# Each 128-column product issued as two 64-column products in the two column halves of the matrix engine

## The chip, the cores and the metric

The kernel runs on one core of a Trainium2 chip. The metric is the device time of one execution in microseconds (us): the median of three runs. A core has a matrix engine (TensorE, PE in the profile), three engines for element-wise work (VectorE is DVE, ScalarE is ACT, GpSimd is POOL) and queues for transfers (DMA). The matrix engine holds a *stationary* operand, which a load (PEld) brings into its array, and streams a *moving* operand past it; the results go to PSUM.

## The reference

An attention block without softmax, then a mixture of four experts over its output. All is float32.

```python
# q, k, v: (8, 8, 576, 64); x: (4608, 512); w1: (4, 512, 1024); w2: (4, 1024, 512)
kv  = np.einsum('bhsd,bhse->bhde', k, v)
out = np.einsum('bhsd,bhde->bhse', q, kv)
rms = np.sqrt(np.mean(out * out, axis=-1, keepdims=True) + 1e-06)
attn = (out / rms * g_norm).astype(np.float32)
x = np.ascontiguousarray(attn.transpose(0, 2, 1, 3)).reshape(B * S, H * D)

p = domain_probs / (domain_probs.sum(-1, keepdims=True) + 1e-09)
out = np.zeros((N, D), dtype=np.float32)
for e in range(E):
    h = np.maximum(x @ w1[e], 0.0)
    out += p[:, e:e + 1] * (h @ w2[e])
```

Nearly all the arithmetic is in `x @ w1[e]` and `h @ w2[e]`.

## The kernel before

Python code first records all operations of the kernel (`plan.add`), each with an estimated cost for the engine it may run on, and a planner (`Plan.layout`) then lays them out: it fixes which engine does what, in which order, and in which buffer. The estimated costs steer only this order; they don't appear in the program. The work is cut into 36 steps, `s = e * 9 + c`: four experts `e` by nine chunks `c` of 512 rows. During the first nine steps (the first expert) the attention of the next batch runs between the products; the later 27 steps hold products alone.

Both large products are computed by a fast matrix multiplication (seven products in place of eight, in two levels for most steps), so the operands are sums and differences of blocks that the element-wise engines make ahead. A float32 product is issued by one call and shows as two records in the profile (two passes); a transpose shows as one.

The products that the change touches, with the shapes that matter (`P` is 128, `HN` 256, `NT` 512, `D` 64):

```python
def pe(products, columns, passes=2):                  # the planner's cost of products
    return {"PE": passes * products * (0.008 + 0.0008125 * columns) + 0.003}

# first product, two levels (steps 1 to 35), L962: 128 stationary, 128 moving columns
for i, m in enumerate(OUTER):                         # seven outer products
    for j, mm in enumerate(ORDER):                    # seven inner ones
        def product(eng, m=m, mm=mm, ps=ps):
            for u in range(2):
                nc.tensor.matmul(
                    ps.ap[:, u * P:(u + 1) * P],
                    lhsT=w1f[e][m][mm][1]()[:, u * P:(u + 1) * P], rhs=views[m][mm][1](),
                    start=(mm in (1, 5) and u == 0), stop=True, skip_group_check=True,
                )
        # ... ACT copies or DVE adds the bank's result into SBUF

# first product of step 0, plain, L1049: 512 moving columns
for kt in range(2):
    nc.tensor.matmul(
        bank.ap[:], lhsT=two(w.ap[:])[:, kt, ut * P:(ut + 1) * P],
        rhs=two(xh[dh].ap[:])[:, kt, :], ...)

# second product, one level (step 0, most of steps 1 to 7, step 35), L1179: 256 moving columns
for kt in range(4):
    nc.tensor.matmul(
        ps.ap[:, 0:HN], lhsT=four(h[m])[:, kt // 2, t, kt % 2, :],
        rhs=w2f[e][m].ap[:, kt * HN:(kt + 1) * HN], ...)

# second product, two levels (steps 8 to 34, a part of steps 1 to 7), L1262: 128 moving columns
for o, m in enumerate(group):
    b, at = forms[m][mm]
    for kt in range(2):
        col = at * HN + kt * P
        nc.tensor.matmul(
            ps.ap[:, o * P:(o + 1) * P], lhsT=b.ap[:, col:col + P],
            rhs=w2q[e][m][mm][1]()[:, kt, :], ...)
```

The attention, which the change leaves as it is, uses the array in parts already. Its products in the first nine steps (`...` marks cuts):

```python
# L683, batch 0 alone: q transposed by products of 64 stationary columns, in both column halves
for r in range(NR):
    for o in range(2):
        at = (o * NR + r) * D
        nc.tensor.matmul(
            bank.ap[o * D:(o + 1) * D, rs], lhsT=qt.ap[:, at:at + D], rhs=ident[:])
# L679, the other batches: full-array transposes of q
nc.tensor.transpose(bank.ap[:, rs], qt.ap[:, rs], ident[:])
# L702: k by v, 64 stationary and 64 moving columns, column half r
nc.tensor.matmul(
    bank.ap[r * D:(r + 1) * D, o * D:(o + 1) * D], lhsT=ks[r], rhs=vs[r], ...)
# L729 and L791: q by kv, in quarters of the array (64 rows, 64 columns)
nc.tensor.matmul(
    raw[r].ap[c * D:(c + 1) * D, ...], lhsT=qTs[hp].ap[half, at:at + D],
    rhs=kv.ap[half, o * D:(o + 1) * D])
# L747: full-array transposes of the attention's result; L773 and L807: transposes of 64 rows
# L1425: transposes of the identity, which keep PE at work while it would wait at the start
```

Of the kernel before, what the change touches and what calls it, by code (L numbers as in the profile page):

```python
# [234 lines left out]
def kernel(  # L235
# [36 lines left out]
    nc = tc.nc  # L272

    B, H, S, D = q.shape
    E, DM, F = moe_w1.shape
    P = nc.NUM_PARTITIONS
# [5 lines left out]
    HN = NT // 2  # L282
# [56 lines left out]
    plan = Plan()  # L339

    def pe(products, columns, passes=2):
        return {"PE": passes * products * (0.008 + 0.0008125 * columns) + 0.003}

    def dve(n):
        return {"DVE": 0.155 + 0.00104 * n}
# [65 lines left out]
    def two(ap):  # L411
        return ap.rearrange("p (k t) -> p k t", k=2)
# [519 lines left out]
    def up(s, e, views):  # L932
        made = {}
        h = {}

        def add(key, to, a, b, op=ALU.add, where=either):
            combine(
                key, where(2 * NT), lambda: to.ap[:], lambda: a.ap[:], lambda: b.ap[:], op,
                [a, b], [to],
            )  # L940

        def relu(key, b):
            plan.add(
                key, act(2 * NT),
                lambda eng: nc.scalar.activation(out=b.ap[:], in_=b.ap[:], func=ACT.Relu),  # L945
                reads=[b], writes=[b],
            )

        for i, m in enumerate(OUTER):
            n = f"{s}_{m}"  # L950
            whole = made[m] = Buf("big", f"m{n}")
            bank = {
                1: Buf("u1", f"u1_{n}"), 2: Buf("u2", f"u2_{n}"), 5: Buf("u2", f"u3_{n}"),
            }
            snap = {}
            for j, mm in enumerate(ORDER):
                key = s + (i + j / 7) / 7
                ps = bank[{2: 2, 5: 5, 3: 5}.get(mm, 1)]

                def product(eng, m=m, mm=mm, ps=ps):  # L960
                    for u in range(2):
                        nc.tensor.matmul(  # L962
                            ps.ap[:, u * P:(u + 1) * P],
                            lhsT=w1f[e][m][mm][1]()[:, u * P:(u + 1) * P], rhs=views[m][mm][1](),
                            start=(mm in (1, 5) and u == 0), stop=True, skip_group_check=True,
                        )

                op = plan.add(
                    key, pe(2, P), product,
                    reads=w1f[e][m][mm][0] + [views[m][mm][0]] + ([ps] if mm == 2 else []),  # L970
                    **{"parts" if mm == 2 else "writes": [ps]},
                    after=last[-2:-1] if mm == 1 else seeds if mm == 5 else (),
                )
                op.marks, op.seed = (ps, HN), mm == 2
                if mm == 3:
                    last.append(op)

                def copy(to, where, ps=ps, key=key):
                    return plan.add(
                        key - 0.4, act(HN),  # L980
                        lambda eng: nc.scalar.activation(  # L981
                            out=where(), in_=ps.ap[:, 0:HN], func=ACT.Copy),
                        reads=[ps], parts=[to],
                    )

                def total(a, t, src, add_, whole=whole, key=key):
                    plan.add(
                        key - 0.4, dve(HN),
                        lambda eng: nc.vector.tensor_tensor(  # L989
                            out=block(whole, a, t), in0=src.ap[:, 0:HN], in1=add_.ap[:], op=ALU.add),  # L990
                        reads=[src, add_], parts=[whole],
                    )

                if mm == 1:
                    seeds = [copy(bank[2], lambda b=bank[2]: b.ap[:, 0:HN])]
                elif mm in (6, 7):
                    snap[mm] = Buf("snap", f"s{mm}_{n}")
                    copy(snap[mm], lambda b=snap[mm]: b.ap[:])
                if mm == 2:
                    copy(whole, lambda whole=whole: block(whole, 0, 0))  # L1000
                elif mm == 7:
                    total(1, 1, bank[5], snap[7])
                elif mm == 4:
                    copy(whole, lambda whole=whole: block(whole, 1, 0))
                elif mm == 3:
                    total(0, 1, ps, snap[6])
            key = s + (i + 1) / 7

            def unit(f):
                h[f] = Buf("big", f"h{f}_{s}")  # L1010
                return h[f]

            if m == 2:
                add(key, unit(1), made[1], made[2])
                relu(key, h[1])
            elif m == 6:
                add(key, made[1], made[1], made[6])
            elif m == 5:
                add(key, made[6], made[1], made[5])
            elif m == 3:  # L1020
                add(key, unit(21), made[6], made[3])
                relu(key, h[21])
                add(key, unit(7), h[1], h[21], ALU.subtract)
            elif m == 7:
                add(key, made[1], made[1], made[7])
                add(key, unit(4), made[1], made[5], where=dve)
                relu(key, h[4])
                add(key, unit(5), h[21], h[4], where=dve)
                add(key, unit(6), h[5], h[1], ALU.subtract, dve)
            elif m == 4:  # L1030
                add(key, unit(2), made[1], made[4])
                relu(key, h[2])
                add(key, unit(3), h[2], h[6], ALU.subtract)
        hidden[s] = h

    def up_plain(s, e, c, key, span):
# [4 lines left out]
        for i in range(8):  # L1041
            uh, a, u = i // 4, i // 2 % 2, i % 2
            bank = Buf("u1" if a == 0 else "u2", f"up{s}_{i}")
            for dh in range(2):
                w, low = corners[uh, dh]

                def product(eng, w=w, bank=bank, dh=dh, ut=2 * a + u):
                    for kt in range(2):
                        nc.tensor.matmul(  # L1049
                            bank.ap[:], lhsT=two(w.ap[:])[:, kt, ut * P:(ut + 1) * P],  # L1050
                            rhs=two(xh[dh].ap[:])[:, kt, :], start=(dh == kt == 0),
                            stop=(dh == kt == 1), skip_group_check=True,
                        )

                op = plan.add(
                    key - 0.89 + 0.01 * (i ^ 2) if i < 4 and dh == 0 else key + span * i / 8,
                    pe(2, NT), product,
                    reads=[w, low, xh[dh]], **({"parts": [bank]} if dh else {"writes": [bank]}),
                )
                op.marks = bank, NT  # L1060
            for th, n in enumerate((1, 21) if uh == 0 else (2, 4)):
                plan.add(
                    key + span * i / 8, act(HN),
                    lambda eng, bank=bank, b=h[n], a=a, u=u, th=th: nc.scalar.activation(
                        out=four(b)[:, a, :, u, :], in_=two(bank.ap[:, th * HN:(th + 1) * HN]),
                        func=ACT.Relu,
                    ),
                    reads=[bank], parts=[h[n]],
                )
# [89 lines left out]
    def down(s, e, c, mixed=False):  # L1159
# [6 lines left out]
        for t in range(2):  # L1166
            banks = {}
            for j, m in enumerate(order):
# [7 lines left out]

                def product(eng, m=m, t=t, ps=ps):
                    for kt in range(4):
                        nc.tensor.matmul(  # L1179
                            ps.ap[:, 0:HN], lhsT=four(h[m])[:, kt // 2, t, kt % 2, :],  # L1180
                            rhs=w2f[e][m].ap[:, kt * HN:(kt + 1) * HN],
                            start=(m in (1, 2, 5) and kt == 0), stop=(kt == 3),
                            skip_group_check=True,
                        )
# [22 lines left out]
    def down_deep(s, e, c, groups=((1, 6), (7, 5), (4, 2), (3,)), base=None, h=None, merge=None, send=None):  # L1207
# [10 lines left out]
        for i, group in enumerate(groups):  # L1218
# [34 lines left out]
            for j, mm in enumerate(ORDER):  # L1253
# [3 lines left out]
                def product(eng, group=group, mm=mm, ps=ps, forms=forms):  # L1257
                    for o, m in enumerate(group):
                        b, at = forms[m][mm]
                        for kt in range(2):  # L1260
                            col = at * HN + kt * P
                            nc.tensor.matmul(  # L1262
                                ps.ap[:, o * P:(o + 1) * P], lhsT=b.ap[:, col:col + P],
                                rhs=w2q[e][m][mm][1]()[:, kt, :],
                                start=(mm in (1, 5) and o == 0 and kt == 0), stop=(kt == 1),
                                skip_group_check=True,
# [117 lines left out]
    for e in range(E):  # L1384
        for c in range(NCH):
# [19 lines left out]
            if s >= 1:  # L1405
                if not primed:
                    banks = [Buf("ab", f"prime{i}") for i in range(2)]

                    def prime(eng, banks=banks):
                        for b in banks:  # L1410
                            nc.tensor.matmul(b.ap[:, 0:P], lhsT=ident[:], rhs=ident[:], start=True,
                                             stop=False, skip_group_check=True)
                            nc.tensor.matmul(b.ap[:, P:HN], lhsT=ident[:], rhs=ident[:], start=False,
                                             stop=True, skip_group_check=True)

                    primed.append(plan.add(s + 1.1, pe(4, P), prime, writes=banks))
                    primed[0].marks = banks[0], HN
# [58 lines left out]
```

## Time and profile before

| | before |
|---|---|
| time, median of 3 runs | 1712.36 us (1711.51 to 1712.5) |
| span of the profiled execution | 1710.4 us |
| PE busy | 1700.4 us (99%) |
| DVE, ACT, POOL busy | 1276.0, 982.5, 715.0 us |
| PE records | 15630 products, 15630 loads |
| 128-column products: L962 | 6860 records in six groups |
| 128-column products: L1262 | 5684 records |

How to read it: the profile gives each engine's busy time and, for each group of instructions (line, engine, operation, output and inputs, shape), the count and the mean length. PE's records overlap: a product's record begins when it starts and ends when its result is through, while the next has long begun. So the length of a PE record is no cost; the distance from one start to the next is. The timeline shows groups in order of time with start, length from first start to last end, and count. "128*64" in a shape is rows by columns of the stationary operand, "128x128" behind it is the moving one.

### The profile page before, as it was taken

Reading aid. Unit: us, or ns where it says so; the run is one execution under the profiler, and the core shown is the slowest. Engines: PE = TensorE matmul, PEld = TensorE weight load, DVE = VectorE, ACT = ScalarE, POOL = GpSimd, SP = SyncE. Lnnn points to the kernel's source line nnn. Section 1 sums busy time; section 2 is a strip of 40 time slices with the busy share of each in tenths; the row PEclk is TensorE's granted clock in tenths of the full one; section 3 lists DMA queues with packets and bytes.
Section 4 is the critical chain, followed back from the end, with each engine's and each line's share of the span. In section 5 each row is a group of like instructions: output and inputs, shape, how many; then the busy total and the mean of one; then the engine's idle time right before and its main releaser. Section 6 shows DMA issues by size and latency. Waiting matters only on the chain.

```text
span 1710.4 us, 39615 instructions
## 1 busy us (share of the span) xinstructions
PE 1700.4 (99%) x15630; PEld 1647.5 (96%) x15630; DVE 1276.0 (75%) x2040; ACT 982.5 (57%) x2405; POOL 715.0 (42%) x677
## 2 busy tenths in 40 slices
PE   9999999999999999999999999999999999999998
PEld 6799999999999999999999999999999999999998
DVE  4855776677698787777788777777788887777774
ACT  3455555455456656665666666656566566656562
POOL 3634331323554543333355465333345544433331
PEclk9999999999999999999999999999999999999999
DMA  9964643544466344444577444444478444444442
GB/s 227 252 203 145 195 145 97 167 152 157 148 172 155 106 101 115 104 115 105 139 174 177 111 112 112 103 110 111 124 185 196 106 107 112 112 112 112 108 103 50
DMA packets 172225, 232.55 MB, mean 136 GB/s; under 512 B 61576, under 2 KB 112648, under 8 KB 172040
## 3 DMA queue, kind: packets, MB, share of 16 engines
q1 hardware_dynamic: 148968, 193.32, 37.3%
q0 software_dynamic: 23072, 36.71, 14.4%
q8 instruction: 123, 2.02, 0.5%
q14 instruction: 62, 0.51, 0.1%
HBM read 155.79 MB, written 74.19 MB: 134 GB/s over the span
## 4 chain that ended last, share of the span: by engine, by line
PE 97%; DVE 1%; DMA 1%; POOL 0%; issue 0%; SPq 0%; ACT 0%
PE u L962 45%; PE db L1262 23%; PE ab L1262 14%; PE db L1179 8%; PE u L1049 2%; PE ab L702 1%; DMA small<-in_q_dram 1%; PE ab L747 1%; PE ab L679 1%; DVE big L1131 1%; PE ab L729 1%; PE u L1179 1%; PE ab L1179 0%; PE ab L791 0%; POOL rt L587 0%
## 5 line engine op out<-in xcount | busy, mean ns | idle before, releaser
L365 DVE TENSOR_TENSOR big<-big,big 128x1024 f32<-128x1024 f32 (+1 forms) x537 | 506.5, 962 | 29.9 <-ACT big L945 15.2
L962 PE MATMUL u<-xf,big 128*128 128x128 f32 x3392 | 491.8, 275 | 0.0
L962 PEld LDWEIGHTS u<-xf,big 128*128 128x128 f32 x3392 | 435.9, 192 | 2.2
L962 PE MATMUL u<-xf,w1y 128*128 128x128 f32 x2652 | 391.5, 276 | 0.0
L989 DVE TENSOR_TENSOR big<-u,snap 128x256 f32<-128x256 f32 x462 | 194.3, 421 | 214.8 <-PE u L962 142.4
L962 PEld LDWEIGHTS u<-xf,w1y 128*128 128x128 f32 x2652 | 342.7, 192 | 1.9 <-DVE big L989 0.2
L981 ACT ACTIVATE snap<-u 128x256 f32<-128x256 f32 x490 | 187.5, 383 | 190.7 <-PE u L962 153.2
L365 POOL TENSOR_TENSOR big<-big,big 128x256 f32<-128x256 f32 (+1 forms) x168 | 215.9, 1299 | 168.2 <-DVE big L365 66.2
L981 ACT ACTIVATE big<-u 128x256 f32<-128x256 f32 x462 | 176.7, 383 | 103.3 <-PE u L962 72.9
L1262 PE MATMUL db<-big,big 128*128 128x128 f32 x1516 | 205.9, 275 | 0.0
L1262 PEld LDWEIGHTS db<-big,big 128*128 128x128 f32 x1516 | 187.3, 192 | 0.1
L365 POOL TENSOR_TENSOR big<-big 128x512 f32<-128x512 f32 (+1 forms) x87 | 105.5, 1215 | 142.2 <-DVE big L365 86.4
L1179 PE MATMUL db<-big,big 128*128 128x256 f32 x696 | 164.6, 380 | 0.0
L1290 ACT ACTIVATE snap<-db 128x256 f32<-128x256 f32 (+1 forms) x230 | 82.2, 357 | 116.8 <-PE db L1262 111.4
L945 ACT ACTIVATE big<-big 128x1024 f32<-128x1024 f32 x132 | 138.6, 1050 | 4.0 <-DVE big L365 3.3
L1179 PEld LDWEIGHTS db<-big,big 128*128 128x128 f32 x696 | 125.9, 191 | 13.9 <-DVE big L596 0.3
L1298 DVE TENSOR_TENSOR big<-ab,snap 128x256 f32<-128x256 f32 x164 | 69.1, 421 | 61.2 <-ACT snap L1290 29.9
L1328 POOL TENSOR_TENSOR big<-big 128x512 f32<-128x512 f32 x25 | 31.8, 1270 | 194.6 <-DVE big L365 174.9
L981 ACT ACTIVATE u<-u 128x256 f32<-128x256 f32 x245 | 90.9, 371 | 28.3 <-PE u L962 11.0
L1147 POOL DMA_DIRECT2D out_dram<-big x94 | 86.0, 1029 | 47.6 <-ACT big L1124 27.6
L365 DVE TENSOR_TENSOR big<-big 128x512 f32<-128x512 f32 (+1 forms) x120 | 105.4, 889 | 0.6 <-PE db L1179 0.6
L1262 PE MATMUL db<-kv,big 128*128 128x128 f32 x644 | 94.5, 275 | 0.0
(197 smaller groups left out, 2716.5 us busy)
## 6 DMA issues: line engine op xcount, KB each, us to landing
xf<-x SPq DMA_DIRECT2D x108, 512.0 KB, 3.7
out_dram<-big POOLq DMA_DIRECT2D x82, 256.0 KB, 5.8
xf<-x_h SPq DMA_DIRECT2D x81, 256.0 KB, 3.1
xf<-x SPq DMA_DIRECT2D x81, 256.0 KB, 3.5
x<-xf SPq DMA_DIRECT2D x36, 512.0 KB, 4.3
big<-in_moe_w_dram SPq DMA_DIRECT2D x31, 512.0 KB, 5.5
x_h<-big SPq DMA_DIRECT2D x18, 512.0 KB, 4.2
big<-in_moe_w_dram POOLq DMA_DIRECT2D x17, 512.0 KB, 6.1
```

Source lines behind the costliest of these rows:

```text
L365: lambda eng: adder(eng).tensor_tensor(out=out_(), in0=a(), in1=b(), op=op),
L945: lambda eng: nc.scalar.activation(out=b.ap[:], in_=b.ap[:], func=ACT.Relu),
L962: nc.tensor.matmul(ps.ap[:, u * P:(u + 1) * P], lhsT=w1f[e][m][mm][1]()[:, u * P:(u + 1) * P], rhs=views[m][mm][1](), start=(mm in (1, 5) ...
L981: lambda eng: nc.scalar.activation(out=where(), in_=ps.ap[:, 0:HN], func=ACT.Copy),
L989: lambda eng: nc.vector.tensor_tensor(out=block(whole, a, t), in0=src.ap[:, 0:HN], in1=add_.ap[:], op=ALU.add),
L1049: nc.tensor.matmul(bank.ap[:], lhsT=two(w.ap[:])[:, kt, ut * P:(ut + 1) * P], rhs=two(xh[dh].ap[:])[:, kt, :], start=(dh == kt == 0), stop ...
L1147: nc.gpsimd.dma_start(out=dst, in_=cell(i)[parts, :], accum_op=ALU.add)
L1179: nc.tensor.matmul(ps.ap[:, 0:HN], lhsT=four(h[m])[:, kt // 2, t, kt % 2, :], rhs=w2f[e][m].ap[:, kt * HN:(kt + 1) * HN], start=(m in (1, ...
L1262: nc.tensor.matmul(ps.ap[:, o * P:(o + 1) * P], lhsT=b.ap[:, col:col + P], rhs=w2q[e][m][mm][1]()[:, kt, :], start=(mm in (1, 5) and o == ...
L1290: lambda eng: nc.scalar.activation(out=where(), in_=group_of(ps.ap), func=ACT.Copy),
L1298: lambda eng: nc.vector.tensor_tensor(out=cell(tq, dq), in0=group_of(src.ap), in1=group_of(add_.ap), op=ALU.add,),
L1328: lambda eng: adder(eng).tensor_tensor(out=whole(to), in0=whole(a), in1=whole(b), op=ALU.add),
```

## The change

Every product with 128 stationary columns becomes two, each with 64 of these columns and with the output in the matching half of the PSUM partitions. The moving operand is the same for both. The aim is that each half of the array loads and streams on its own, so that one half's change of operand lies under the other's stream. The planner's cost of products is changed with it. Transposes and the attention's products stay as they were.

```diff
     def pe(products, columns, passes=2):
-        return {"PE": passes * products * (0.008 + 0.0008125 * columns) + 0.003}
+        return {"PE": passes * products * (0.0025 + columns / 1200.0) + 0.003}
+
+    def halves_of(out_, lhsT, rhs, **kw):
+
+        for half in range(2):
+            cols = slice(half * D, (half + 1) * D)
+            nc.tensor.matmul(out_[cols], lhsT=lhsT[:, cols], rhs=rhs, **kw)
@@ the first product, two levels
                     for u in range(2):
-                        nc.tensor.matmul(
+                        halves_of(
                             ps.ap[:, u * P:(u + 1) * P],
-                            lhsT=w1f[e][m][mm][1]()[:, u * P:(u + 1) * P], rhs=views[m][mm][1](),
+                            w1f[e][m][mm][1]()[:, u * P:(u + 1) * P], rhs=views[m][mm][1](),
                             start=(mm in (1, 5) and u == 0), stop=True, skip_group_check=True,
                         )
@@ the same edit in the plain first product (L1049), in both second products (L1179, L1262)
@@ and in the two pairs of priming products that clear two PSUM banks once
```

The planner's cost moves from 0.112 to 0.109 us for a pass of 128 columns and from 0.216 to 0.216 for 256, so the order it lays out changes in places as well.

More of the change, by code (lines that the diff above doesn't have):

```diff
@@ L1048, in product @@
                     for kt in range(2):
-                        nc.tensor.matmul(
-                            bank.ap[:], lhsT=two(w.ap[:])[:, kt, ut * P:(ut + 1) * P],
+                        halves_of(
+                            bank.ap[:], two(w.ap[:])[:, kt, ut * P:(ut + 1) * P],
                             rhs=two(xh[dh].ap[:])[:, kt, :], start=(dh == kt == 0),
@@ L1178, in product @@
                     for kt in range(4):
-                        nc.tensor.matmul(
-                            ps.ap[:, 0:HN], lhsT=four(h[m])[:, kt // 2, t, kt % 2, :],
+                        halves_of(
+                            ps.ap[:, 0:HN], four(h[m])[:, kt // 2, t, kt % 2, :],
                             rhs=w2f[e][m].ap[:, kt * HN:(kt + 1) * HN],
@@ L1261, in product @@
                             col = at * HN + kt * P
-                            nc.tensor.matmul(
-                                ps.ap[:, o * P:(o + 1) * P], lhsT=b.ap[:, col:col + P],
+                            halves_of(
+                                ps.ap[:, o * P:(o + 1) * P], b.ap[:, col:col + P],
                                 rhs=w2q[e][m][mm][1]()[:, kt, :],
@@ L1410, in prime @@
                         for b in banks:
[L1411 to L1414, printed above, removed]
+                            halves_of(b.ap[:, 0:P], ident[:], rhs=ident[:], start=True,
+                                      stop=False, skip_group_check=True)
+                            halves_of(b.ap[:, P:HN], ident[:], rhs=ident[:], start=False,
+                                      stop=True, skip_group_check=True)
                     primed.append(plan.add(s + 1.1, pe(4, P), prime, writes=banks))
```

## The prediction

> **What bounds the kernel now.** I read the page first: busy shares, slices, chain. TensorE (PE) is busy 99% of the span, its clock is granted in full throughout, and the chain that ended last is 97% PE, nearly all of it the three product lines L962, L1262 and L1179.
>
> ```profile
> PE 1700.4 (99%) x15630; PEld 1647.5 (96%) x15630; DVE 1276.0 (75%) x2040; ACT 982.5 (57%) x2405; POOL 715.0 (42%) x677
> PEclk9999999999999999999999999999999999999999
> PE 97%; DVE 1%; DMA 1%; POOL 0%; issue 0%; SPq 0%; ACT 0%
> ```
>
> There are 15630 PE records for 7994 products in the program: a float32 product is two records (two passes), a transpose one. So the time is the number of passes times the distance between two starts, and only that distance can move the end. A record's own length (275 ns) says nothing of it, since records overlap. I took the distance from the count of records in stretches that hold nothing but 128-column products (columns: stretch, then busy time and records of each engine, granted clock, DMA):
>
> ```profile
> 600.00:700.00 100.00, 100.00 (x898) 100.00 (x898) 76.38 (x118) 59.92 (x151) 37.42 (x36) 1.00 0.46 110
> 480.00:1660.00 1180.00, 1179.97 (x10542) 1179.00 (x10541) 930.07 (x1458) 726.48 (x1811) 519.46 (x482) 1.00 0.51 126
> ```
>
> In the first row, 898 records less the 2.5 that began before the stretch (275/112): 100 us / 895.5 = 111.7 ns. The second row is 69% of the span with no PE gap worth a name.
>
> What will the new form cost? The kernel already holds it in one place: the first transposes of q (L683) are products of 64 stationary columns that alternate between the two column halves, 128 moving columns each, two passes each, just as the change issues all products. The timeline of PE around one such run (start, length, group, count):
>
> ```profile
> 12.72 1.09 PE L683 MATMUL ab<-ident,small 128*64 128x128 f32 x16 [0.68 <-DMA small<-in_q_dram]
> 13.75 0.69 PE L729 MATMUL u<-kv,small 64*64 64x64 f32 x32
> 14.37 0.88 PE L1425 MATMUL ab<-ident 128*128 128x128 f32 x6
> 15.18 0.34 PE L702 MATMUL ab<-big,big 96*64 96x64 f32 x4
> ```
>
> Sixteen half passes: the last starts 1.09 - 0.273 (one record's length) = 0.817 us after the first, so 0.817/15 = 54.5 ns each; from the starts of the twelve in the middle of the run I get 0.655/12 = 54.6. A pair of halves, which does the work of one full pass, takes 109.2 ns. The halves do run side by side: one alone needs 128 moving columns, about 107 ns.
>
> The third thing to look at is what it costs PE to go from one shape of product to another, because the attention's small products are scattered between the large ones in the first 480 us:
>
> ```profile
> 126.73 0.61 PE L962 MATMUL u<-big,w1y 128*128 128x128 f32 x4
> 127.27 1.16 PE L729 MATMUL ab<-kv,small 64*64 64x64 f32 x64
> 128.36 0.71 PE L962 MATMUL u<-big,big 128*128 128x128 f32 x4
> 128.91 0.38 PE L1179 MATMUL db<-big,big 128*128 128x256 f32 x1
> ...
> 142.04 0.60 PE L679 MATMUL ab<-ident,small 128*128 128x128 f32 x4
> 142.57 1.39 PE L702 MATMUL ab<-kv 120*64 120x64 f32 x40
> 143.89 0.38 PE L962 MATMUL u<-xf,big 128*128 128x128 f32 x1
> ```
>
> Four full passes before L729 take 127.27 - 126.73 = 0.54 us instead of 4 x 0.1117 = 0.447: leaving a full-array run costs 0.093. Four after it take 0.55: entering costs another 0.10.
>
> **What the Trainium skill says.** "TensorEngine Tiling (Array Packing)", Key Properties: tiles of the array load and multiply independently, but a change of the tiling mode drains the engine. The trace agrees with both: halves at 54.6 ns, and the 0.09 to 0.10 us at each change above. "TensorE: Matmul & The Clock Gate", LDWEIGHTS: a load takes the stationary columns divided by 1.2 GHz, so 107 ns for 128 and 53 for 64. The load records agree in their difference (192 ns with 128 columns, 137 with 64: 55 ns for 64 columns), and it offers a reason why full passes need 111.7 ns: load and stream are equally long there and each load follows the last. That reason is my reading, not measured. Same page, Back-to-back issue gap: a fixed 2.5 ns a product; the trace has about 2.5 more than 128/1.2 for the pair of halves, 216 ns against 213.3 for 256 columns, and 429 against 426.7 for 512, but 5 for full passes of 128. So only the 128-column products have anything to give.
>
> **The change part by part.**
>
> 1. *Products with 128 moving columns.* L962: 3430 and L1262: 2842 products, times two passes = 12544 passes. Each goes from 111.7 to 109.2: 12544 x 2.5 ns = **-31 us**.
>
> 2. *Products with 256 moving columns* (L1179, 392 products, 784 passes). The program's timeline has 16 of them in a row over 3.46 us, 216 ns each. As two halves by the same rule, 213.3 + 2.5 = 216 (an estimate). **0.** The 512-column products of the first stage (64 passes, 429 ns) likewise **0**. The four priming products are nothing.
>
> 3. *Changes of shape.* In the instruction order of the two programs I counted the runs of one shape on PE. Before: 56 full-array runs (products together with transposes), 19 of column halves (L683, L702), 26 of quarter arrays (L729, L791), 16 of row halves; 116 changes. After: the products join the column halves, so the runs of L702 merge with them, but each group of transposes (still full-array) is now cut off: 54 full-array runs, 79 of column halves, 26 and 16 as before; 174 changes. The cost of a run, in and out, beyond its passes:
>  - full array, products first: 0.093 + 0.101 = 0.194 us (above);
>  - full array, transposes first: L1425's six take 15.18 - 14.37 = 0.81 where six at 109 ns are 0.654: 0.15;
>  - column halves: L683's run takes 13.75 - 12.72 = 1.03 where 16 x 0.0546 is 0.874: 0.15; L702's takes 143.89 - 142.57 = 1.32 where 40 at 30 ns are 1.20: 0.12.
>
>  Before: 46 x 0.194 + 10 x 0.15 + 19 x 0.12 = 12.7 us. After: 54 x 0.15 + 79 x 0.15 = 20 us less a little for the few that still end in L702: 19.8. The other shapes cost the same. **+7 us**, all of it in the first 480 us.
>
> 4. *Instructions.* PE's records go from 15630 to about 29000, loads as well. L729 is the densest stretch there is: 64 records and 64 loads in 1.09 us with the change of shape, 7.5 ns an instruction inside; the new form needs one per 27 ns. **0.**
>
> 5. *The other engines* do the same work. The planner, whose cost for a product moves by 2 to 3%, orders it anew; the lists have 14 additions more on VectorE and 18 operations fewer on GpSimd. In the stretch from 480 to 1660 us VectorE is busy 930 of 1180 us; with PE done in 1180 - 10542 x 0.0025 = 1154 us that is 81% instead of 79%. It doesn't become the bound.
>
> PE lies on the path nearly everywhere, so the parts add: -31 + 0 + 7 = **-24 us**, 1712.4 - 24 = **1688 us**, or 1.4% less.
>
> **The rivals.**
>
> *The loads of the two halves queue behind each other in long runs.* Then a pair would take two loads of 64 columns in turn. L702 gives the load-bound distance, since its stream is also only 64 columns: 30 ns per half pass, so 60 for the pair. Were they in turn, 60 would be one load and a full pair 120: 12544 x 8 = +104 us, about 1820. But 60 ns for the pair, with each half's load alone worth 53 or more, says they go in parallel, and L683 says the same. The doubt left is that L683's runs are 16 records long and lie in the first 20 us, with other engines idle.
>
> *Instruction supply.* Twice the instructions for as long as 1.7 ms; the instruction queue moved only 2.02 MB in 123 packets before, and would move about 4. L729's 128 in a row show how fast PE takes them, not how long. In the first 60 us DMA is nearly full (97% busy), so a late fetch there would stop PE. If a few per cent of the fetches came late, some 10 to 30 us would be lost and the change would be worth nothing.
>
> *New waits from the new order.* By the list of waits PE now waits 5 us in all, most of it in the first 66 us. The start is a chain of loads and small steps; a different order there can cost or save some us. Down to 5 or up to 15 lost makes 1684 to 1695.
>
> *The fixed part vanishes.* If the overlap of halves hid the 2.5 ns as well, a pair would take 107 ns: 12544 x 4.7 = -59, +7: 1660. L683's 109.2 speaks against it.
>
> **Range and chances.** The terms uncertain by a few us are the distance (0.3 ns either way is 4 us), the changes of shape (twice as dear for halves: +10; free: -10) and new waits (+5 to +15). That gives 1679 to 1702, lopsided upward. The 2% line for faster is 1678, just below; it would need cheaper changes of shape and no new wait at once: 0.11. Slower by over 2% needs the first or second rival in force: 0.06.
>
> **What would show it.** In a stretch of the later experts the new program should have 100/0.0546 = 1830 half passes in 100 us and advance the same products in 97.8% of the time; the stretch 480 to 1660 should shrink by some 26 us and the first 480 us by about nothing (L962 and L1262 save 5 there, shape changes give back 7). A transpose group between products should take about 0.3 us more than its passes. I am wrong if the pair of halves is not 109 ns, if PE shows idle time with "issue" or a semaphore as its releaser beyond 480 us, or if the early stage moves by more than 8 us.

## The result and the profile after

The changed kernel takes 1691.44 us (median of 4 runs, 1690.61 to 1695.65) against 1712.11 us for the kernel before: a ratio of 0.9886, 95% interval 0.9872 to 0.99 (the two medians alone give 0.9879). That is 1.2% less, under the 2% line. The prediction was 1688, in a range of 1679 to 1702.

The page after, with the lines that answer to those of before (engines, clock, instruction queue, the chain):

```profile
PE 1676.0 (99%) x29030; PEld 1570.2 (93%) x29030; DVE 1252.0 (74%) x2054; ACT 982.8 (58%) x2405; POOL 732.5 (43%) x663
PEclk9999999999999999999999999999999999999999
q8 instruction: 228, 3.74, 0.9%
PE 95%; DVE 2%; POOL 1%; DMA 1%; issue 0%; ACT 0%; POOLq 0%; ACTq 0%; SPq 0%; DVEq 0%
```

PE is still busy 99% of the span and still carries the chain, now with nearly twice the records. The distance between starts is what moved. The two stretches shown of before, in the kernel after (busy time and records of PE, PEld, DVE, ACT, POOL; granted clock; DMA):

```profile
600.00:700.00 100.00, 100.00 (x1836) 100.00 (x1834) 76.56 (x121) 59.89 (x152) 44.97 (x41) 1.00 0.46 115
480.00:1660.00 1180.00, 1175.49 (x21442) 1170.72 (x21440) 926.09 (x1478) 736.32 (x1839) 533.82 (x485) 1.00 0.51 127
```

1836 records less the 5 that began before the stretch: 100 us / 1831 = 54.6 ns for a half pass, 109.2 for the pair that replaces a pass of 111.7. That is L683's figure to the digit, in runs of thousands. The 54.6 is a mean: single starts stand in pairs, 6 to 7 ns apart, with 102 to 103 ns to the next pair, and so do the loads. So the two halves change their operands at the same time, and not one under the other's stream, as was aimed at; what has become shorter is the load of each, which the run with 96 columns below takes up. The second row shows what is not as before: PE was idle for 0.03 us from 480 to 1660 and is idle for 4.5 us now.

The shapes, from PE's timeline (lines are shifted by 6: L685 is before's L679, L708 its L702, L735 its L729; L348 is every split product):

```profile
126.51 0.61 PE L348 MATMUL u<-big,w1y 128*64 128x128 f32 x8
127.04 1.16 PE L735 MATMUL ab<-kv,small 64*64 64x64 f32 x64
128.13 0.66 PE L348 MATMUL u<-big,big 128*64 128x128 f32 x8
128.62 3.62 PE L348 MATMUL db<-big,big 128*64 128x256 f32 x32
...
140.82 1.90 PE L348 MATMUL db<-big,big 128*64 128x256 f32 x16
142.65 0.66 PE L685 MATMUL ab<-ident,small 128*128 128x128 f32 x4
143.24 1.39 PE L708 MATMUL ab<-kv 120*64 120x64 f32 x40
144.45 0.61 PE L348 MATMUL u<-xf,big 128*64 128x128 f32 x8
144.99 0.46 PE L779 MATMUL ab<-ident,small 64*128 64x64 f32 x4
```

Eight half passes are worth 0.437 us. Before L735 they take 0.53 (leaving costs 0.09), after it 0.49 (entering costs 0.05). Four transposes (L685) take 0.59, where they took 0.53 before: they now change shape at both ends. Between L708 and the half products there is no change of shape: 143.24 to 144.45 is 1.21 us for 40 passes at 30 ns, where the same run took 1.32 before. The 32 half passes of 256 columns take 3.45 us from 128.62 on (their length less the 0.38 of the last record, and one more distance of 0.21), where 16 full ones took 3.46.

To see where the 20 us went, I read the same points of the work in both traces: where, by count, the first products of steps 1, 9 and 35 begin, and the end of the last product.

| stretch | before, us | after, us | difference |
|---|---|---|---|
| to step 1 | 64.6 | 63.9 | -0.7 |
| steps 1 to 8 (attention beside) | 430.6 | 430.0 | -0.6 |
| steps 9 to 34 | 1139.2 | 1120.1 | -19.1 |
| step 35 to the end | 71.2 | 70.2 | -1.0 |

Steps 9 to 34 have 26 x 392 = 10192 passes; at 2.5 ns they should give 25.5 us. They gave 19.1. Adding up what single distances have beyond the usual, PE lost 0.6 us in waits there before and 7.0 after: the missing 6.4. The two largest, in the chain of the kernel after (start, us, what):

```profile
501.72 4.97 DVE big L1137 x4
506.69 0.34 DVE big L995
...
896.45 10.71 DMA out_dram<-big
```

At 505 us PE loses 1.6 us behind a burst of VectorE; at 907 us it loses 1.8 us behind a result transfer that held its buffer for 10.7 us, where 5.8 was the median of such transfers before.

### The profile page after: what moved, and what is told of

It is laid out like the page before. It is cut to its first block, busy times and chain, and to the rows that moved or that the text cites. A ratio compares the mean times of both kernels' runs of the same rounds, so it can differ in the third digit from the quotient of the medians.

```text
span 1688.8 us, 66409 instructions
## 1 busy us (share of the span) xinstructions
PE 1676.0 (99%) x29030; PEld 1570.2 (93%) x29030; DVE 1252.0 (74%) x2054; ACT 982.8 (58%) x2405; POOL 732.5 (43%) x663
## 4 chain that ended last, share of the span: by engine, by line
PE 95%; DVE 2%; POOL 1%; DMA 1%; issue 0%; ACT 0%; POOLq 0%; ACTq 0%; SPq 0%; DVEq 0%
PE u L348 45%; PE db L348 31%; PE ab L348 14%; PE ab L708 1%; PE ab L753 1%; PE ab L685 1%; PE ab L735 1%; DVE big L1137 1%; DMA out_dram<-big 1%; POOL rt L593 1%; DVE big L371 1%; PE ab L1431 0%; DVE tot L400 0%; POOL xf L371 0%; PE ab L689 0%
## 5 line engine op out<-in xcount | busy, mean ns | idle before, releaser
L348 PE MATMUL u<-xf,big 128*64 128x128 f32 x6784 | 486.7, 273 | 2.2 <-ACT snap L987 2.1
L348 PEld LDWEIGHTS u<-xf,big 128*64 128x64 f32 x6784 | 393.0, 137 | 7.5 <-ACT snap L987 3.2
L348 PE MATMUL u<-xf,w1y 128*64 128x128 f32 x5304 | 391.7, 273 | 2.1 <-DVE big L995 1.5
L348 PE MATMUL db<-big,big 128*64 128x128 f32 (+1 forms) x4336 | 365.7, 307 | 0.3 <-DVE big L602 0.3
L371 POOL TENSOR_TENSOR big<-big,big 128x256 f32<-128x256 f32 (+1 forms) x194 | 251.4, 1303 | 256.8 <-DVE big L371 128.8
L348 PEld LDWEIGHTS u<-xf,w1y 128*64 128x64 f32 x5304 | 309.1, 137 | 7.1 <-DVE big L995 1.7
L348 PEld LDWEIGHTS db<-big,big 128*64 128x64 f32 x4336 | 265.6, 137 | 40.7 <-DVE big L602 0.5
L1130 ACT ACTIVATE big<-big,p_all 128x256 f32<-128x256 f32 x206 | 97.9, 501 | 5.7 <-POOL big L1334 5.3
L348 PE MATMUL db<-kv,big 128*64 128x128 f32 x1360 | 99.1, 273 | 0.0
L348 PE MATMUL ab<-big,big 128*64 128x128 f32 (+1 forms) x1360 | 96.7, 278 | 0.0
```

The source lines that it names most:

```text
L348: nc.tensor.matmul(out_[cols], lhsT=lhsT[:, cols], rhs=rhs, **kw)
L371: lambda eng: adder(eng).tensor_tensor(out=out_(), in0=a(), in1=b(), op=op),
L1130: lambda eng: nc.scalar.activation(out=cell(i, half), in_=ap(), func=ACT.Copy, scale=prob()),
```

## The experiments

Eleven runs. They ask four things: is the gain the pass distance or the planner's new order; why is a full pass 111.7 ns; what do changes of shape cost; where do the new waits come from, and can the kernel be had without them. The first two runs take the change apart: the planner's cost alone, and the split alone.

### The planner's cost alone

```diff
 def pe(products, columns, passes=2):
-    return {"PE": passes * products * (0.008 + 0.0008125 * columns) + 0.003}
+    return {"PE": passes * products * (0.0025 + columns / 1200.0) + 0.003}
```

> The kernel before with nothing but the planner's new cost of products (no product split). Theory of the pass distance: the gain of the change comes from PE's start-to-start distance alone, so this run stays at the kernel before's time, 1712 +- 5 us, with a pass still at 111.7 ns. Rival (the new order of operations carries a part of the gain): 1700 us or less.

Measured: 1717.5 us, ratio 1.0034 (1.0021 to 1.0047), half a microsecond above the 1712 +- 5. PE, DVE, ACT and POOL have their operations in the order of the changed kernel. The pass stays at 111.7 ns, and the kernel is 6 us slower. The stretch 480 to 1660 us, with 2.65 us of idle PE where the kernel before had 0.03:

```profile
480.00:1660.00 1180.00, 1177.35 (x10497) 1174.75 (x10496) 902.55 (x1457) 727.17 (x1805) 526.79 (x482) 1.00 0.50 125
```

And two pieces of its chain (start, us, what):

```profile
502.41 4.85 DVE big L1131 x4
507.25 0.35 DVE big L989
```

The wait at 505 us of the changed kernel is here too, behind the same four operations of VectorE, in a kernel without one split product. Waits from step 9 to 34 are 5.5 us against 0.6 before. So the new order doesn't carry the gain; it brings most of the waits. To the start of step 9 it takes 0.9 us off (494.3 us against 495.2).

### The split alone, in the old order

```diff
-    return {"PE": passes * products * (0.0025 + columns / 1200.0) + 0.003}
+    return {"PE": passes * products * (0.008 + 0.0008125 * columns) + 0.003}
```

(against the changed kernel: all products stay split)

> All products split into column halves, but the planner keeps the cost and so the order of the kernel before. Theory of the pass distance: 12544 passes by 2.5 ns saved (-31), the changes of shape cost +7, so 1688; if the 5 to 7 us of waits that the changed kernel has after 480 us come from the new order, they are gone here and the time is 1684 to 1688, below the changed kernel's 1691.4. Rival (the waits come from PE being faster, whatever the order): 1690 to 1693. Rival (the order carries the gain): near 1700 or more.

Measured: 1691.5 us, ratio 0.9883 (0.9868 to 0.9897): the same as the changed kernel, while PE, DVE, ACT and POOL have their operations in the order of the kernel before. So the split alone carries the gain. The stretch 480 to 1660 us, with 2.5 us of idle PE:

```profile
480.00:1660.00 1180.00, 1177.47 (x21496) 1174.17 (x21494) 962.15 (x1480) 741.53 (x1844) 528.00 (x487) 1.00 0.51 128
```

The parts differ. Steps 9 to 34 take 1116.2 us, 4 less than in the changed kernel, with 3.1 us of waits instead of 7.0; step 9 begins at 499.3 us, 5.5 later. So my expectation about the waits held for the late steps, but the time missed the 1684 to 1688 and lies where the first rival had it. Of the 5.5 us, 3.4 lie before the first product of the first expert: in this execution PE stood still there for 1.95 us with no releaser shown (0.8 in the changed kernel), and then its granted clock was 0.50 for 3.4 us, which costs 1.7. I can't put that on the order. Waits that PE's own speed brings, in an unchanged order, are the 2.5 us between 0.6 and 3.1.

### Only the late products split

```diff
-    def halves_of(out_, lhsT, rhs, **kw):
+    def halves_of(out_, lhsT, rhs, late=False, **kw):
+        if not late:
+            nc.tensor.matmul(out_, lhsT=lhsT, rhs=rhs, **kw)
+            return
         for half in range(2):
 ...
+                            late=s >= NCH,          # first product: steps 9 to 35
 ...
+                            late=s >= NCH - 1,      # both second products: steps 8 to 35
```

(with the old planner cost)

> Old planner cost; only the products of steps 9 to 35 (first product) and 8 to 35 (second product), which have no attention beside them, are split. 10584 of the 12544 passes keep their gain of 2.5 ns (-26.5 us), and the transposes in the first steps stay in one shape with the products. Theory that the early halves are eaten by changes of shape: about 1686 to 1688, 1 to 3 us better than the same kernel with all products split. Rival (changes of shape cost nothing to speak of, early halves are worth their 4.5 us): 3 to 5 us worse than with all split.

Measured: 1689.8 us, ratio 0.9875 (0.9858 to 0.9891). 1.8 us better in the medians, as expected, but the intervals of the two overlap. The order of operations is the same in both. What is clear: leaving 1960 early passes unsplit, 4.9 us by their distance, cost nothing. Steps 1 to 8 took 430.9 us here and 431.9 with all split.

### The transposes in column halves as well

To test the cost of a change of shape I took its cause away. The kernel is the split in the old order, with

```diff
-                            nc.tensor.transpose(bank.ap[:, rs], qt.ap[:, rs], ident[:])
+                            halves_of(bank.ap[:, rs], qt.ap[:, rs], rhs=ident[:], start=True, stop=True)
 ...
-                        nc.tensor.transpose(
-                            bank.ap[:, rs], x.ap[:, o * NT + r * P:o * NT + (r + 1) * P], ident[:])
+                        halves_of(
+                            bank.ap[:, rs], x.ap[:, o * NT + r * P:o * NT + (r + 1) * P],
+                            rhs=ident[:], start=True, stop=True)
```

> All products split, planner's costs and order of the kernel before, and now the attention's 240 full-array transposes of batches 1 to 7 and of the attention's result are issued as products by the identity in column halves too, as batch 0's are. That doubles their passes (+240 x 109 ns = +26 us) but leaves 50 runs of the full array and 39 of the halves fewer in the order. Theory that each run costs about 0.15 us to enter and leave: -13 us, so +13 against the same kernel with transposes, 1704. Rival (changes of shape cost nothing to speak of): +26, 1718.

Measured: 1702.2 us, ratio 0.9944 (0.9924 to 0.9964), 10.7 more than the same kernel with transposes. Passes account for +26.2, so 89 runs fewer gave back 15.5 us: 0.17 us a run, against my 0.15; the medians are sure to some 2 us, so it may be 0.15 to 0.20. PE's timeline shows turned blocks standing among products with no seam, 16 half passes in 0.87 to 0.88 us:

```profile
143.97 1.04 PE L348 MATMUL ab<-ident,small 128*64 128x128 f32 x16
144.84 1.04 PE L348 MATMUL ab<-ident,big 128*64 128x128 f32 x16
145.72 0.61 PE L348 MATMUL u<-xf,big 128*64 128x128 f32 x8
```

### A full pass with 96 stationary columns

Why does a full pass need 111.7 ns and a pair of halves 109.2? In the kernel before, every second product of L1262 gets a quarter of its stationary columns less; that quarter of its output is left out.

```diff
-                                ps.ap[:, o * P:(o + 1) * P], lhsT=b.ap[:, col:col + P],
+                                ps.ap[0:P - 32 * kt, o * P:(o + 1) * P],
+                                lhsT=b.ap[:, col:col + P - 32 * kt],
```

> The kernel before (full-array products), but every second product of the second layer's two-level form loads and computes only 96 of its 128 stationary columns, so a quarter of that product's output is left out; 2842 of the passes are concerned. Theory that a full pass needs 111.7 ns because its load of 128 columns is as long as the stream: a pass with 96 columns starts 109.2 ns after the one before it, while one with 128 keeps 111.7; the whole about 7 us faster, 1705. Rival (the 2.5 ns belong to the full-array shape or to the two-pass product, whatever the load's length): 111.7 for all, 1712.

Measured: 1706.2 us in one run, and, clearer, the distances: over some 2800 passes each, 111.7 ns after the start of a pass with 128 columns and 109.2 after one with 96. The excess goes with the width of the operand, not with the full-array shape: 96 columns are no half and no tile. One detail went against my words: the excess stands after the start of the wide pass, not before it. A load's record begins 2 to 3 ns after the start of the pass before its own, so the load that stands in such a gap can be a narrow one. If a product is stamped when it is taken up and then still waits for its own load, that is what one would see, but no record shows it; the wide products' records are 275 ns long, the narrow ones' 272 to 273. The run narrows a pass's load and its output together. What tells them apart are transposes and products with 256 moving columns. The rows of before, then those of this run (operation, shortest, median and longest record):

```profile
L1262 PEld LDWEIGHTS db<-small,big x568: 191/192/193, 516.1 to 1673.9; 128*128 128x128 f32 x190
L747 PEld LDWEIGHTS ab<-ident,big x128: 138/141/144, 18.4 to 402.2; 128*128 128x128 f32 x128
L747 PE MATMUL ab<-ident,big x128: 272/273/329, 18.5 to 402.3; 128*128 128x128 f32 x128
```

```profile
L1262 PEld LDWEIGHTS db<-small,big x568: 163/178/192, 515.7 to 1668.0; 128*128 128x128 f32 x95, 128*96 128x96 f32 x95
L1262 PE MATMUL db<-small,big x568: 272/274/275, 515.8 to 1668.1; 128*128 128x128 f32 x95, 128*96 128x128 f32 x95
```

A transpose has 128 stationary columns and a full output too, in one pass, but its load records are 141 ns long, not 192, and transposes follow each other at 109. Loads are 163 ns with 96 columns, 137 with 64. And with 256 moving columns, when the stream is twice as long as the load, a full pass had 216.1 - 213.3 = 2.8 over its stream, not 5. By the records' difference, 55 ns for 64 columns, a load of 128 takes about 110 ns (an estimate), and a stream of 128 takes 107. So wherever the load is shorter than the stream, the excess is 2.5 to 2.8, and only where they are about equal is it 5.

### Halves issued one after the other

The changed kernel, with L1179's products in another order:

```diff
-                    for kt in range(4):
-                        halves_of(ps.ap[:, 0:HN], four(h[m])[:, kt // 2, t, kt % 2, :], ...)
+                    for half in range(2):
+                        cols = slice(half * D, (half + 1) * D)
+                        for kt in range(4):
+                            nc.tensor.matmul(ps.ap[cols, 0:HN],
+                                lhsT=four(h[m])[:, kt // 2, t, kt % 2, cols], ...)
```

> The changed kernel, with one line altered: the one-level second product (784 of the full passes) issues all its four column-half products of one half and then the four of the other, instead of alternating. Theory that the halves save by running side by side, and do so only with the neighbour in the order: of 16 half passes in a row only two pairs (at the turns) can overlap, so 14 streams of some 214 ns in place of 8 distances of 216, 784/8 x (3.0 - 1.73) = +124 us, about 1815. Rival (a half pass costs 54.6 or 108 ns by itself, whatever stands beside it): 1691.

Measured: 1751.5 us in one run, 60 more than the changed kernel. The direction is that of halves that need each other; the amount is half of what I reckoned. PE's timeline around one such group:

```profile
152.75 2.81 PE L1187 MATMUL db<-big,big 128*64 128x256 f32 x16
155.49 0.66 PE L685 MATMUL ab<-ident,small 128*128 128x128 f32 x4
```

16 half passes take 155.49 - 152.75 - 0.09 = 2.65 us, 12.3 streams of 216 ns and not 14. The starts step by 216 ns four times, then stand in four close pairs (5 to 57 ns apart), then step by 216 again. I read this as the second half beginning beside the fifth of the first half's eight passes, so four of them overlap at the turn; where the group stands among other products, its records mix with theirs as well. On 98 groups the loss is 60/98 = 0.61 us each. A half pass alone costs its whole stream, 216 ns here.

### Quarters

```diff
-        for half in range(2):
-            cols = slice(half * D, (half + 1) * D)
+        for half in range(4):
+            cols = slice(half * 32, (half + 1) * 32)
```

(against the changed kernel)

> The changed kernel, but each product as four of 32 stationary columns in four column quarters: the same streams, twice the instructions again (about 56000 records and as many loads). Theory that only the stream and 2.5 ns bind: four quarter passes take 109.2 ns, 1691 +- 6. Rival (PE's supply of instructions is near its limit at one per 27 ns, with one per 13.6 ns needed here): 5% slower or more, with PE's idle time put down to issue.

Measured: 1976.4 us in one run, 17% slower. The profile page's instruction queue, the list of waits (line, releaser, us in total, times, longest), PE's timeline around one such wait, and the stretch behind it (the third figure from the end is the granted clock):

```profile
q8 instruction: 437, 7.16, 1.5%
```

```profile
PE u L348 <- issue: 80.1, 84, 3.6
PE db L348 <- issue: 70.5, 61, 3.3
PE ab L348 <- issue: 39.6, 35, 3.6
```

```profile
691.37 0.62 PE L348 MATMUL db<-kv,big 128*32 128x128 f32 x16
694.77 0.86 PE L348 MATMUL db<-kv,big 128*32 128x128 f32 x12 [2.79 <-issue]
```

```profile
694.80:698.20 3.40, 3.40 (x68) 3.04 (x72) 1.87 (x3) 0.38 (x1) 0.00 (x0) 0.50 0.02 5
```

Between waits four quarters do take 109.2 ns, so the array would allow it. But PE stands still 180 times for 190 us, and in the trace nearly all of those stops are 128 loads apart or a multiple of it, to within three: 256 instructions, one packet of the instruction queue (7.16 MB / 437 = 16 KB). At full pace a packet would last 256 x 13.65 = 3.5 us, and the packets came 4.1 us apart in the median. After the stop of 2.79 us the next 16 groups took 213 ns each instead of 109, at a granted clock of 0.50. The trace has 18 such stretches, 65 us together, each behind a stop of 2.0 to 3.6 us; at half pace that is some 32 us of the 285 lost. About 60 us are neither in the stops nor in these stretches; I did not break them down. So supply was a real limit; the halves need a packet each 7 us (median 7.1) and stay under it.

### Can the waits be planned away?

The kernel with late halves, with one number of the planner altered in each run:

```diff
-                            op.end += 9.0 if op.kb == 512 else 5.5
+                            op.end += 11.0
```

> The kernel with only the late products split and the old planner cost, with one number of the planner altered: it reckons 11 us for the landing of an accumulating transfer of GpSimd, where it reckoned 5.5 (results) and 9 (weights). Theory that the waits of PE at the change of experts (about 3 us there, behind result transfers that took 8 to 11 us and held their buffers) come from that reckoning: they go, and the time is 1685 to 1688. Rival (the buffers are short there whatever the planner knows, or the waits move to other places): 1689 to 1695.

```diff
-    ... passes * products * (0.008 + 0.0008125 * columns) + 0.003
+    ... passes * products * (0.0065 + 0.0008125 * columns) + 0.003    # then 0.0095, then 0.011
```

> The kernel with only the late products split; the planner reckons 110.5 ns for a pass of 128 columns in place of 112 (the chip takes 111.7 for full passes and 109.2 for pairs of halves). Theory that the few us of waits are an accident of each order and that only the pass distance is lawful: passes unchanged, time anywhere in 1686 to 1696. Rival (a planner that takes PE for slower than it is leaves the other engines slack, and one that takes it for faster brings waits): slower than with 112, 1692 to 1696.

> As the run before, with 113.5 ns in the planner. Accident of order: anywhere in 1686 to 1696. Rival (a slower PE in the plan leaves slack): faster than with 112, 1686 to 1689.

> As the runs before, with 115 ns in the planner. Accident of order: anywhere in 1686 to 1696. Rival (a slower PE in the plan leaves slack): the fastest of the four, 1685 to 1688.

| planner | time, us | ratio (95% interval) | lost beyond the pass distance in steps 9 to 34, us |
|---|---|---|---|
| as before (112 ns) | 1689.8 | 0.9875 (0.9858 to 0.9891) | 3.1 |
| transfers reckoned at 11 us | 1690.5 | 0.9869 (0.9853 to 0.9886) | 4.8 |
| 110.5 ns | 1693.0 | 0.9888 (0.9873 to 0.9903) | 7.7 |
| 113.5 ns | 1689.1 | 0.9867 (0.9852 to 0.9882) | 4.4 |
| 115 ns | 1697.9 | 0.9919 (0.9902 to 0.9935) | 7.1 |

In all rows but the last, 0.9 us of the last column is nine changes of shape where full and half products meet. Reckoning the transfers longer did not help, as the rival had it: the waits moved. The four pass costs give 1693.0, 1689.8, 1689.1, 1697.9, with no trend; at 115 ns most of the 8 us more is lost by the start of step 9 (503.9 us against 495.0). 115 ns lies a little outside the 1686 to 1696 I gave to accident. The rival that a slower PE in the plan leaves slack fits 110.5 and about fits 113.5, but it had 115 as the fastest of the four, and that is the slowest. The spread from order alone is some 9 us, which is why the changed kernel's own 3 us above the prediction cannot be put on the halves. No version here is clearly faster than the changed kernel: the best, 1689.1, overlaps it in its interval.

## Why the prediction was right

**The pass distance.** Step 1 of the sum stood on 54.6 ns read from 16 records; the stretch 600 to 700 us has 54.6 from 1831. The doubt that short runs at the start might not speak for long ones fell. Steps 9 to 34 became 19.1 us shorter with 6.4 us more of waits: 25.5 us on 10192 passes, 2.5 ns each, which makes 31 us on 12544, as worked out. The planner's cost alone made the kernel 6 us slower, and the split in the old order was as fast as the changed kernel, so the gain is the split's.

The rule that the prediction takes from the Trainium skill for this distance ("TensorE: Matmul & The Clock Gate", Back-to-back issue gap) divides the moving columns by 2.4 GHz when the clock is granted in full. The passes here don't: at a granted clock of 1.00 they take (429 - 216)/256 = 0.83 ns a column, which is 1.2 GHz. The prediction reckoned with 1.2 GHz without showing where it comes from; of the rule, the fixed 2.5 ns agrees with the trace.

**The 256- and 512-column products.** Reckoned as 0; 16 of them took 3.46 us before and their 32 halves take 3.45 now.

**Changes of shape.** Reckoned as 0.15 us for a run of halves or of transposes: the timeline shows 0.09 + 0.05, and the transposes in halves gave 0.17 a run, from the totals. The +7 was of the right size: in the old order, the way from the first product of the first expert to the start of step 9 took 2.6 us longer than before (474.2 against 471.6), where -5 and +7 give +2. The new order alone took 1.0 off this way, and the changed kernel needed 0.5 more for it. That the early stage came out "by about nothing", at -1.3 us, has luck in it: the changed kernel's execution reached that first product 1.9 us sooner (21.7 us against 23.6), and there the executions of these kernels differ by up to 3.4 us (21.7 to 25.1).

**The instructions.** "0" held for halves, but my ground for it was weak. I took L729's 7.5 ns an instruction for the pace that PE can take. It is the pace of 128 instructions, half a packet; the quarters show that a sustained 13.65 ns cannot be fed. The rival that I gave 10 to 30 us was closer than it looked: the halves need a packet each 7 us, and with quarters one came each 4.1, a factor of 1.7.

**The term that was mis-sized** is the new waits. They were a rival ("down to 5 or up to 15 lost"), left out of the central sum. They came to +6.4 us in steps 9 to 34, 2.5 of it from PE's own speed in the old order and the rest with the new order; the first stage came out at -1.3 where I had about +2, and took part of it back. By stretches: -25.5 + 6.4 - 1.3 - 1.0 = -21.4 on the trace, -20.7 by the measured times, for -24 predicted. Idle time of PE behind a semaphore beyond 480 us was on my list of what would show a step wrong, and it is there, 4.5 us of it. I had expected such waits from the chain of loads at the start; the large ones stood at 505 us and from 907 to 974 us, in the first steps of the second and third expert, the two largest behind a VectorE burst and a result transfer. VectorE, busy 926 of the 1180 us (78%, where I had 81%), was not the bound, but it is not free at every moment.

**The reason for the 111.7 ns** was marked as a reading. The 96-column run, the transposes and the 256-column products support it: the excess is there only where load and stream are about equally long. They do not show the mechanism inside the array, and the excess appears one pass later than I had put it.

## What to carry to other kernels

Where a stationary operand is used for a single stream of no more columns than it has itself, look at the distance between starts, not at record lengths: if it exceeds that of halves measured in the same kernel, splitting the operand over two column halves can be worth the difference, here 2.2% of the distance and 1.2% of the kernel. Issue the halves alternately, count the runs of one shape that the split creates or removes, at about 0.15 us each for entering and leaving, and look at how long a packet of instructions lasts before splitting further. In a planned kernel, run the planner's new constants without the change before crediting either: here they alone cost 6 us and moved unrelated waits about.

## What was not expected of the hardware

- Instruction supply: PE stopped 180 times, 190 us in all, with four quarters at 13.65 ns an instruction; packets of 256 instructions came 4.1 us apart in the median. With one per 27.3 ns, in the changed kernel, the stops without a releaser were two, 1.0 us in all, both before the first split product.
- After a stop of 2.79 us PE took 213 ns instead of 109 for 16 groups of quarters, 3.4 us long and at a granted clock of 0.50, then went back to 109. A stop of 1.95 us in the split with the old order was followed by 3.4 us at 0.50 too.
- Entering the full array with products cost 0.10 us, with transposes 0.055, column halves 0.053; leaving the full array or the halves costs 0.09.
- A transpose's load records last 141 ns where a product's with the same 128 x 128 shape last 192, and only after the latter does the next pass start at 111.7 ns instead of 109.
